# Blocks of 120 tokens laid end to end over the batches, weight chunks in one transfer, taps zeroed at batch starts

## The chip, the core and the metric

The kernel runs on one core of a Trainium2 chip. The metric is the device time of one launch in microseconds (us). Five engines work side by side, each through its own instructions in program order: PE (TensorE, matrix multiplies and transposes), DVE (VectorE), ACT (ScalarE), POOL (GpSimd) and SP (SyncE, which here only issues transfers). Transfers between DRAM and on-chip memory run on 16 DMA engines.

## The reference

Two steps follow each other. The first is a dynamic convolution: for each of 8 x 4160 tokens, eight heads of 24 channels each mix the last seven tokens (the taps) with softmaxed weights; before a batch's first token stand zeros. The second picks, in each batch, the 128 tokens of highest score, sends them through two expert matrices and adds the gated result.

```python
w = np.exp(weight_gen - max); w = w / (w.sum(-1) + 1e-9)          # (8, 4160, 8 heads, 7 taps)
x_pad = concat([zeros(B, 6, D), x], axis=1)                       # D = 192
out[b, s, h] = sum over k of w[b, s, h, k] * x_pad[b, s + k, h]   # 24 channels per head
scores = out @ w_gate
for b in range(8):
    top = argpartition(-scores[b], 128)[:128]
    ye = relu(out[b, top] @ w1) @ w2                              # 192 -> 1024 -> 192
    out[b, top] += sigmoid(scores[b, top])[:, None] * ye
```

## The kernel before

**Windows and blocks.** The output is cut into windows of `W` = 120 tokens. A window reads 128 rows of x: its 120 tokens and the six before them. Each batch has `NW` = 35 windows, the last with 80 tokens, so there are `TOT` = 280 windows, and `U` = 4 of them form one of `NU` = 70 blocks. A block of x is loaded by SP (`load_x`, L158) into one of `NST` = 5 staging tiles `xst`, cast to 16 bits by POOL (`cast_x`, L168) into one of `XR` = 24 tiles `x`, and there the six rows before a batch start are zeroed (L174).

**Weights.** The windows fall into three groups of two, three and three batches (70, 105 and 105 windows). In a group a window is a partition, and its tokens lie along the row, in five chunks of 24 tokens. `load_w` (L217) loads a chunk with two transfers for each batch, of 32 and of 3 partitions. For a chunk ACT computes the exponential (`sm_exp`, L235), DVE (first group) or POOL (`sm_den`, L249 or L252 to L256) the sum over taps, ACT its reciprocal (`sm_r`, L262 and L264), and DVE multiplies (`sm_norm`, L274). PE transposes the result (L293), and DVE or ACT copy it out as `wt` (L304, L306).

**The loop.** In iteration `s`, DVE builds the banded matrix of block `s + 2` (`band`, L728), PE multiplies block `s` (`conv`, L754), ACT copies block `s - 1` out of PSUM as `co` (L777), and SP stores it (`put`, L767). Beside that PE transposes x (`y_t`, L320) 1.49 blocks per iteration, so that all scores are known at iteration 46, long before block 69 is convolved; the transposed x is copied out (L329, L331) and multiplied by the gate (L343 to L349). After the scores come the search for the top 128 (DVE), and for each batch a gather, the experts and a scatter.

**The order.** It is written out by hand. `feed` issues loads of x and, once five are ahead, a cast; before the loop it is called until `XA` = 16 blocks are loaded and 11 cast. In the loop the loads are spread evenly up to iteration 43, and `cast_to` keeps the casts ahead of the transposes. `SM1`, `WT1`, `SM2` and `WT2` are the iterations of the softmax steps and weight transposes of the second and third groups. Each engine keeps this order: an instruction that waits holds everything behind it on its engine. Transfers from SP and ACT draw on eight completion semaphores in turn, so the queue also waits for the transfer that had the same semaphore before.

Of the kernel before, what the change touches and what calls it, by code (L numbers as in the profile page):

```python
# [33 lines left out]
XR = 24  # L34
# [8 lines left out]
def kernel(  # L43
# [17 lines left out]
    NW = -(-S // W)  # L61
    LAST = S - (NW - 1) * W
    TOT = B * NW
    NU = TOT // U
    assert NU * U == TOT
    GROUPS = ((0, 2), (2, 5), (5, 8))
    NWG = 3 * NW

# [31 lines left out]
def fast_path(  # L100
    ctx, tc, x_flat, wg_flat, moe_w_gate, moe_w1, moe_w2, out_flat, sc_d, cand_d, flag_i,
    B, S, F, CAP, N, SP, PPB, NW, LAST, TOT, NU, GROUPS, NWG, MUL,
# [29 lines left out]
    def row0(g):  # L132
        b, i = divmod(g, NW)
        return b * S + i * W - (K - 1)

    xst = {}

    def load_x(u):

        t = xsp.tile([P, U, D], FP32, tag="xst", name="xst")  # L140
        xst[u] = t
        g, end = u * U, (u + 1) * U
        while g < end:
            b = g // NW
            e = min(end, (b + 1) * NW)
            lo, hi = g, e
            if g == 0:
                nc.gpsimd.memset(t[0:K - 1, 0, :], 0.0)
                nc.sync.dma_start(out=t[K - 1:P, 0, :], in_=x_flat[0:P - (K - 1), :])
                lo += 1  # L150
            if e == TOT:
                hi -= 1
                j = hi - u * U
                r = min(P, N - row0(hi))
                nc.gpsimd.memset(t[:, j, :], 0.0)
                nc.sync.dma_start(out=t[0:r, j, :], in_=x_flat[row0(hi):row0(hi) + r, :])
            if hi > lo:
                nc.sync.dma_start(  # L158
                    out=t[:, lo - u * U:hi - u * U, :],
                    in_=ap_of(x_flat, x_flat.offset + row0(lo) * D,  # L160
                              [[D, P], [W * D, hi - lo], [1, D]]),
                )
            g = e

    def cast_x(u):
        t = xp.tile([P, U, D], FP16, tag="x", name=f"x{u}")
        xs[u] = t
        nc.gpsimd.tensor_copy(  # L168
            out=t.rearrange("p u d -> p (u d)"), in_=xst.pop(u).rearrange("p u d -> p (u d)")
        )  # L170
# [26 lines left out]
    def load_w(gi, ci, home=None):  # L197
        b0, b1 = GROUPS[gi]
# [4 lines left out]
        for b in range(b0, b1):  # L203
            p0 = (b - b0) * NW
            n = NW
            if b == B - 1 and t0 + nt > LAST:
                n = NW - 1
                lim = max(0, LAST - t0)
                nc.gpsimd.memset(t[96:(b1 - b0) * NW, 0:nt, :], 0.0)
                if lim > 0:  # L210
                    nc.sync.dma_start(
                        out=t[p0 + n:p0 + n + 1, 0:lim, :],
                        in_=wg_flat[None, b * S + n * W + t0:b * S + n * W + t0 + lim, :],
                    )
            cuts = [0, 32, n]
            for u, v in zip(cuts[:-1], cuts[1:]):
                nc.sync.dma_start(  # L217
                    out=t[p0 + u:p0 + v, 0:nt, :],
                    in_=ap_of(wg_flat, wg_flat.offset + (b * S + u * W + t0) * HK,
                              [[W * HK, v - u], [HK, nt], [1, HK]]),  # L220
                )
# [20 lines left out]

    def sm_den(gi, ci, eng):
# [4 lines left out]
        if eng == "v":  # L248
            nc.vector.tensor_reduce(out=d, in_=av[:, :, :, 0:K], axis=AX.X, op=ALU.add)  # L249
        else:  # L250
# [5 lines left out]
            nc.gpsimd.tensor_tensor(out=d, in0=s4[:, :, :, 0], in1=s4[:, :, :, 1], op=ALU.add)  # L256
        sm[(gi, ci)] = den
# [55 lines left out]
    y16 = ypl.tile([P, TOT, H], FP16, name="y16")  # L313
    ystate = {}

    def y_t(u):
        xf = xs[u].rearrange("p t d -> p (t d)")
        tp = ps_t.tile([P, M, P], FP16, tag="tps", name="xtps")
        for r in range(NT):
# [5 lines left out]
    def y_x(u, eng):  # L325
        tp = ystate.pop(u)
        xT = xtp.tile([P, NT, P], FP16, tag="xT", name="xT")
        if eng == "v":
            nc.vector.tensor_copy(out=xT[:, :, :], in_=tp[:, 0:NT, :])  # L329
        else:  # L330
            nc.scalar.copy(out=xT[:, :, :], in_=tp[:, 0:NT, :])  # L331
        ystate[u] = xT

    def y_d(u, cps, j):
# [4 lines left out]
        for r in range(NT):  # L339
# [12 lines left out]
    def y_e(us, cps):  # L352
        n = len(us) * U
# [10 lines left out]
    def score_t(gi):  # L364
        b0, b1 = GROUPS[gi]
        n = (b1 - b0) * NW
        w0 = b0 * NW
# [39 lines left out]
    def score_m(gi, j):  # L407
        b0, b1 = GROUPS[gi]
# [842 lines left out]
```

## Time and profile before

| | us |
|---|---|
| median of 3 runs | 295.83 (294.73 to 297.66) |
| the profiled execution | 295.27 |
| its span, first to last instruction | 293.5 |
| around the span | 1.8 |

The profile is of one execution. Busy times are those of single engines and overlap. A row's square bracket names the idle time of the engine just before the instruction and what ended it. The mean share of the 16 DMA engines counts the time that packets took, waiting on memory included, so it may pass 1.

### The profile page before, as it was taken

How to read it: one execution, taken by the hardware profiler on the slowest of the kernel's cores; microseconds unless marked ns; L12 is line 12 of the kernel's file. 1: busy time of each engine (PE TensorE's matmuls, PEld its weight loads, DVE VectorE, ACT ScalarE, POOL GpSimd, SP SyncE). 2: the span in 40 equal slices, each digit the busy share in tenths (PEclk: the TensorE clock that was granted, in tenths of full speed). 3: DMA queues.
4: the chain of work that ended last, by engine and by line, in shares of the span. 5: the costliest groups of instructions: out<-in, count | busy, mean ns of one | idle time of the engine just before them, and what ended most of it. 6: DMA issues, size and time to landing. Idle time of an engine off the chain costs nothing.

```text
span 293.5 us, 8921 instructions
## 1 busy us (share of the span) xinstructions
PE 171.8 (59%) x3627; PEld 159.0 (54%) x3627; DVE 226.2 (77%) x242; ACT 170.5 (58%) x331; POOL 155.7 (53%) x199
## 2 busy tenths in 40 slices
PE   0005731647499489464569869577581316679950
PEld 0005731647399489454569859577571214677740
DVE  3798953978979999955777989977989998797100
ACT  2874604869779638676589858665141851436720
POOL 5637339886624219846734533249561933864431
PEclk9999999975969855955557998855555555559965
DMA  3698899899899999997999998785934540747410
GB/s 103 162 273 239 205 272 249 227 337 325 246 308 337 278 256 290 253 256 207 317 322 344 334 310 252 211 270 151 170 87 104 162 135 10 191 129 212 132 40 21
DMA packets 78610, 64.04 MB, mean 218 GB/s; under 512 B 7261, under 2 KB 76718, under 8 KB 78564
## 3 DMA queue, kind: packets, MB, share of 16 engines
q1 hardware_dynamic: 76084, 61.05, 72.2%
q0 software_dynamic: 2032, 2.36, 3.8%
q8 instruction: 30, 0.49, 0.7%
q14 instruction: 16, 0.13, 0.2%
q10 hardware_dynamic: 448, 0.00, 0.1%
HBM read 37.70 MB, written 26.49 MB: 219 GB/s over the span
## 4 chain that ended last, share of the span: by engine, by line
DMA 29%; DVE 19%; PE 17%; POOL 13%; issue 12%; ACT 5%; SPq 1%; ACTq 1%; POOLq 0%; DVEq 0%
DMA xst<-in_x_dram 14%; DMA out_dram<-co 10%; PE sps L414 4%; POOL x L168 4%; PE cps L754 4%; DVE band__163 L728 4%; DVE sp L398 3%; DVE band__161 L728 3%; PE xtps L320 3%; DVE junk L555 3%; POOL s L252 2%; DVE band__162 L728 2%; ACT xT L331 2%; POOL out_dram L709 2%; PE wtps L293 2%
## 5 line engine op out<-in xcount | busy, mean ns | idle before, releaser
L168 POOL CAST x<-xst 128x768 f16<-128x768 f32 x70 | 62.6, 904 | 72.1 <-DMA xst<-in_x_dram 59.7
L777 ACT COPY co<-cps 128x768 f32<-128x768 f32 x70 | 56.1, 806 | 41.1 <-DMA out_dram<-co 17.2
L728 DVE TENSOR_TENSOR band__161<-wt,mask 128x3840 f16<-128x3840 f16 (+1 forms) x24 | 48.9, 2039 | 4.3 <-PE cps L754 4.2
L728 DVE TENSOR_TENSOR band__162<-wt,mask 128x3840 f16<-128x3840 f16 (+2 forms) x24 | 46.9, 1958 | 5.6 <-PE cps L754 5.6
L320 PE MATMUL xtps<-ident,x 128*128 128x128 f16 x420 | 43.7, 270 | 11.4 <-DVE xT L329 6.4
L728 DVE TENSOR_TENSOR band__163<-wt,mask 128x3840 f16<-128x3840 f16 (+2 forms) x24 | 46.4, 1935 | 2.1 <-PE cps L754 2.1
L331 ACT COPY xT<-xtps 128x768 f16<-128x768 f16 x56 | 44.7, 830 | 5.4 <-PE xtps L320 5.4
L320 PEld LDWEIGHTS <-x 128*128 128x128 f16 x420 | 33.9, 122 | 12.0 <-issue 6.6
L754 PE MATMUL cps<-x,band__162 128*128 128x24 f16 x736 | 23.5, 179 | 22.2 <-ACT y L354 16.8
L754 PEld LDWEIGHTS <-band__162 128*128 128x128 f16 x736 | 23.0, 103 | 23.7 <-issue 17.4
L754 PE MATMUL cps<-x,band__163 128*128 128x24 f16 x736 | 23.1, 179 | 15.3 <-ACT y L354 10.3
L754 PEld LDWEIGHTS <-band__163 128*128 128x128 f16 x736 | 22.8, 102 | 16.9 <-issue 15.2
L754 PEld LDWEIGHTS <-band__161 128*128 128x128 f16 x768 | 24.2, 104 | 14.0 <-DVE band__161 L728 9.9
L754 PE MATMUL cps<-x,band__161 128*128 128x24 f16 x768 | 24.4, 180 | 12.5 <-DVE band__161 L728 8.7
L274 DVE TENSOR_TENSOR amem<-amem,r 105x1536 f16<-105x1536 f16 (+1 forms) x15 | 18.2, 1210 | 15.1 <-ACT r L264 15.0
L293 PE MATMUL wtps<-ident,amem 105*128 105x105 f16 (+1 forms) x192 | 14.7, 247 | 23.8 <-DVE amem L274 17.6
L293 PEld LDWEIGHTS <-amem 105*128 105x128 f16 (+1 forms) x192 | 13.1, 125 | 25.0 <-DVE amem L274 18.5
L414 PE MATMUL sps<-sp,ident 105*105 105x240 f16 (+1 forms) x96 | 17.5, 352 | 8.0 <-DVE sp L398 5.7
L235 ACT ACTIVATE amem<-wraw 105x1344 f16<-105x1344 f32 (+1 forms) x13 | 17.1, 1315 | 8.5 <-DMA wraw<-in_weight_gen_dram 5.4
L414 PEld LDWEIGHTS <-ident 105*105 105x105 f16 (+1 forms) x96 | 14.7, 168 | 8.8 <-DVE sp L398 4.3
L398 DVE TENSOR_TENSOR sp<-amem,Y 105x1920 f16<-105x1920 f16 (+1 forms) x12 | 16.9, 1421 | 1.6 <-ACT Y L381 1.6
L252 POOL TENSOR_TENSOR s<-amem 105x768 f32<-105x768 f16 x10 | 14.7, 1466 | 4.7 <-ACT amem L235 4.6
(175 smaller groups left out, 375.7 us busy)
## 6 DMA issues: line engine op xcount, KB each, us to landing
xst<-in_x_dram SPq DMA_DIRECT2D x62, 384.0 KB
out_dram<-co SPq DMA_DIRECT2D x62, 360.0 KB
wraw<-in_weight_gen_dram SPq DMA_DIRECT2D x36, 168.0 KB
xst<-in_x_dram SPq DMA_DIRECT2D x6, 288.0 KB
out_dram<-co SPq DMA_DIRECT2D x4, 270.0 KB
xst<-in_x_dram SPq DMA_DIRECT2D x4, 192.0 KB
out_dram<-co SPq DMA_DIRECT2D x4, 180.0 KB
amem<-in_weight_gen_dram SPq DMA_DIRECT2D x4, 168.0 KB
```

The source lines that it names most:

```text
L168: nc.gpsimd.tensor_copy(out=t.rearrange("p u d -> p (u d)"), in_=xst.pop(u).rearrange("p u d -> p (u d)"))
L235: nc.scalar.activation(out=a_view(gi)[0:n, :, q0:q1, 0:K].rearrange("p c q k -> p q c k"), in_=wr[0:n, 0:nq * M, :].rearrange("p (q m) (h ...
L252: nc.gpsimd.tensor_tensor(out=s4, in0=av[:, :, :, 0:4], in1=av[:, :, :, 4:8], op=ALU.add)
L274: nc.vector.tensor_tensor(out=v, in0=v, in1=r2[0:n, 0:cq, :].rearrange("p (c q) b -> p c q b", q=nq)[:, :, :, None, :] .to_broadcast([n, M ...
L293: nc.tensor.transpose(out=tp[:, m, 0:n], in_=am[0:n, o:o + P], identity=ident16[0:n, 0:n])
L320: nc.tensor.transpose(out=tp[:, r, :], in_=xf[:, r * P:(r + 1) * P], identity=ident16[:, :])
L331: nc.scalar.copy(out=xT[:, :, :], in_=tp[:, 0:NT, :])
L398: nc.vector.tensor_tensor(out=sp[0:n], in0=ap_of(a0, am[0:n, o:o + 1].offset, [list(a0.ap[0]), [2 * H * Q * 8, 2], [Q * 8, H], [1, Q * 8]] ...
L414: nc.tensor.matmul(out=sps[0:n].rearrange("p m q k -> p m (q k)"), lhsT=ident16[0:n, 0:n], rhs=sp[0:n, :, h, :], start=(h == 0), stop=(h = ...
L728: eng.tensor_tensor(out=bt[:, o:o + n * H * BC].rearrange("p (c q m) -> p c q m", q=NQ, m=M), in0=wts[gi][:, l:l + n].rearrange("p w h m - ...
L754: nc.tensor.matmul(out=cps[:, w // 2, (w % 2) * D + h * G:(w % 2) * D + (h + 1) * G], lhsT=bt[:, o:o + P], rhs=xwin(si * U + w)[:, h * G:( ...
L777: nc.scalar.copy(out=co.rearrange("p (j w) d -> p j (w d)", w=2), in_=cts[si][:, :, 0:2 * D],)
```

## The change

Windows run through all 33,280 tokens without regard to batches. There are 278 of them (the last holds 40 tokens), and 70 blocks (the last holds two windows). The groups have 64, 112 and 102 windows. A weight chunk is loaded in one transfer of 64 or 112 partitions; in the third group it is one of 96 and one of 5 or 6, and for four of its chunks (before: two) POOL first zeroes the last rows. Since a window may now hold a batch start, the taps that reach over it are zeroed in the weights after the sum over taps: seven batch starts give six multiplies on DVE (`sm_start`) with masks that POOL builds at the start (`start_masks`). Zeroing x at batch starts goes. `XR` is 23, `XA` 12, and `SM1` and `WT1` are earlier. The gate's loads (`wcol`) are issued first, and x's first loads and the masks stand ahead of the other constants.

```diff
-XR = 24
+XR = 23
-    NW = -(-S // W)
-    LAST = S - (NW - 1) * W
-    TOT = B * NW
-    GROUPS = ((0, 2), (2, 5), (5, 8))
+    TOT = -(-N // W)
+    LAST = N - (TOT - 1) * W
+    NU = -(-TOT // U)
+    GB = (64, 176)
+    GROUPS = ((0, GB[0]), GB, (GB[1], TOT))
...
     def cast_x(u):
-        for j in range(U):
-            if (u * U + j) % NW == 0:
-
-                nc.gpsimd.memset(t[0:K - 1, j, :], 0.0)
...
     def load_w(gi, ci, home=None):
-        for b in range(b0, b1):
-            p0 = (b - b0) * NW
-            n = NW
...
-            cuts = [0, 32, n]
-            for u, v in zip(cuts[:-1], cuts[1:]):
+        n = w1 - w0
+        if w1 == TOT and t0 + nt > LAST:
+            lim = max(0, LAST - t0)
+            nc.gpsimd.memset(t[96:n, 0:nt, :], 0.0)
+            n -= 1
+            if lim > 0:
+                g = (w0 + n) * W + t0
+                nc.sync.dma_start(out=t[n:n + 1, 0:lim, :], in_=wg_flat[None, g:g + lim, :])
+
+        cuts = [0, n // 16 * 16] + ([n] if n % 16 else [])
+        for u, v in zip(cuts[:-1], cuts[1:]):
+            nc.sync.dma_start(
+                out=t[u:v, 0:nt, :],
+                in_=ap_of(wg_flat, wg_flat.offset + ((w0 + u) * W + t0) * HK,
+                          [[W * HK, v - u], [HK, nt], [1, HK]]),
+            )
...
+    def start_masks():
+
+        for (gi, q), ps in starts.items():
+            ts = []
+            for p in ps:
+                t = consts.tile([P, M, 8], FP16, name=f"bm{gi}_{q}_{p}")
+                nc.gpsimd.affine_select(
...
+                nc.gpsimd.affine_select(
...
+    def sm_start(gi, ci, eng):
+        n, q0, q1, nq, col, cq = dims(gi, ci)
+        for q in range(q0, q1):
+            if (gi, q) in bms:
+                v = a_view(gi)[0:n, :, q, :].rearrange("p (m h) k -> p m h k", h=H)
+                eng.tensor_tensor(
+                    out=v, in0=v,
+                    in1=bms[(gi, q)][0:n, :, None, :].to_broadcast([n, M, H, 8]), op=MUL,
+                )
...
             nc.vector.tensor_reduce(out=d, in_=av[:, :, :, 0:K], axis=AX.X, op=ALU.add)
+            sm_start(gi, ci, nc.vector)
...
     def sm_norm(gi, ci):
+        if gi and SE:
+            sm_start(gi, ci, nc.vector)
...
-    XA = 16
+    XA = 12
+    SE = 1
-    SM1 = (0, 1, 3, 5, 7)
-    WT1 = (11, 11, 11, 12, 12, 12, 13, 13)
+    SM1 = (0, 1, 3, 4, 6)
+    WT1 = (9, 9, 10, 10, 11, 11, 12, 12)
...
+    nc.scalar.dma_start(out=wcol[:, 0:1], in_=wgv[0:128, :])
...
     for ci in range(NWC):
         load_w(0, ci, None if ci < 3 else spare[:, ci - 3])
...
+    feed(NST - 1)
+    start_masks()
+    sel_consts()
+    ex_consts()
     gsel = consts.tile([P, 4, H], FP32, name="gsel")
```

**On ACT, at the very start** (`wcol` is the gate, `mask_s` a copy of the band's mask, `amem` the softmax memory), before:

```order
L80 ACT_TABLE_LOAD
L849 COPY mask_s<-mask 128x120
L852 DMA wcol<-in_moe_w_gate_dram 128x1
L853 DMA wcol<-in_moe_w_gate_dram 64x1
L854 DMA wcol<-in_moe_w_gate_dram 64x1
L855 DMA wcol<-in_moe_w_gate_dram 128x1
L235 ACTIVATE amem_128,emax<-wraw 70x3x64x7 x2
```

and with the change:

```order
L79 ACT_TABLE_LOAD
L854 DMA wcol<-in_moe_w_gate_dram 128x1
L855 DMA wcol<-in_moe_w_gate_dram 64x1
L856 DMA wcol<-in_moe_w_gate_dram 64x1
L857 DMA wcol<-in_moe_w_gate_dram 128x1
L889 COPY mask_s<-mask 128x120
L225 ACTIVATE amem_128,emax<-wraw 64x3x64x7 x2
```

The four issues moved from behind the copy of the mask, which waits for PE, to ahead of it.

**On POOL, the casts of x ahead of the second group's first sum over taps** (`s` and `den` are its steps). Before, the last seven of 13 casts stand here:

```order
L168 CAST x_339<-xst 128x768
L168 CAST x_343<-xst 128x768
L168 CAST x_347<-xst 128x768
L174 MEMSET x_347 6x192
L168 CAST x_352<-xst 128x768
L168 CAST x_356<-xst 128x768
L168 CAST x_360<-xst 128x768
L168 CAST x_447<-xst 128x768
L252 TENSOR_TENSOR s_506<-amem_129 105x768
L253 TENSOR_TENSOR s_506<-s_506 105x192x2
L256 TENSOR_TENSOR den<-s_506 105x192
```

and with the change the last three of nine:

```order
L164 CAST x_344<-xst 128x768
L164 CAST x_348<-xst 128x768
L164 CAST x_435<-xst 128x768
L283 TENSOR_TENSOR s_489<-amem_129 112x768
L284 TENSOR_TENSOR s_489<-s_489 112x192x2
L287 TENSOR_TENSOR den<-s_489 112x192
L164 CAST x_495<-xst 128x768
```

Four casts moved from ahead of the sum to behind it.

**On SP, around the third group's first two chunks** (`co` is a finished block, `xst` a load of x), before:

```order
L767 DMA out_dram<-co 120x4x192
L217 DMA wraw<-in_weight_gen_dram 32x1344
L217 DMA wraw<-in_weight_gen_dram 3x1344
L217 DMA wraw<-in_weight_gen_dram 32x1344
L217 DMA wraw<-in_weight_gen_dram 3x1344
L217 DMA wraw<-in_weight_gen_dram 32x1344
L217 DMA wraw<-in_weight_gen_dram 3x1344
L158 DMA xst<-in_x_dram 128x4x192 x2
```

and with the change:

```order
L804 DMA out_dram<-co 120x4x192
L207 DMA wraw<-in_weight_gen_dram 96x1344
L207 DMA wraw<-in_weight_gen_dram 6x1344
L154 DMA xst<-in_x_dram 128x4x192
L804 DMA out_dram<-co 120x4x192
L203 DMA wraw<-in_weight_gen_dram 1x896
L207 DMA wraw<-in_weight_gen_dram 96x1344
L207 DMA wraw<-in_weight_gen_dram 5x1344
L154 DMA xst<-in_x_dram 128x4x192
```

A chunk takes two or three places in the queue where it took six, and the transfers of the second chunk stand behind a zeroing on POOL.

## Rows read from the trace of the kernel before

**Rows 1.** The page: span, busy time by engine, and the DMA share in 40 slices.

```profile
span 293.5 us, 8921 instructions
PE 171.8 (59%) x3627; PEld 159.0 (54%) x3627; DVE 226.2 (77%) x242; ACT 170.5 (58%) x331; POOL 155.7 (53%) x199
DMA  3698899899899999997999998785934540747410
```

**Rows 2.** Stretches of the span: busy us of each engine, granted clock, DMA share, GB/s.

```profile
0.00:20.00 20.00, 0.28 (x1) 0.10 (x1) 13.07 (x18) 12.10 (x25) 9.70 (x36) 1.00 0.63 172
20.00:60.00 40.00, 19.30 (x402) 18.06 (x403) 30.74 (x24) 19.70 (x38) 27.00 (x30) 1.00 0.91 241
60.00:100.00 40.00, 29.64 (x718) 28.41 (x718) 34.27 (x23) 32.57 (x61) 20.78 (x26) 0.79 1.00 309
100.00:140.00 40.00, 25.75 (x530) 24.47 (x530) 32.65 (x26) 24.98 (x50) 22.71 (x26) 0.59 0.91 252
140.00:192.00 52.00, 38.64 (x901) 36.94 (x898) 43.94 (x33) 38.93 (x71) 22.21 (x27) 0.76 0.97 300
192.00:254.00 62.00, 32.08 (x679) 29.33 (x680) 55.35 (x103) 25.36 (x54) 36.62 (x30) 0.50 0.54 136
```

**Rows 3.** The waits: who waited for whom, us in total, times, longest.

```profile
POOL x L168 <- DMA xst<-in_x_dram: 59.7, 36, 5.2
ACT den L262 <- POOL den L256: 14.6, 6, 11.0
PE xtps L320 <- POOL x L168: 5.0, 2, 3.2
```

**Rows 4.** ACT in order of time: start, us, line, operation, idle time before.

```profile
4.72 0.26 ACT L849 COPY mask_s<-mask 128x120 f16<-128x120 f16 x1 [2.62 <-PE mask L848]
4.73 0.39 ACTq L852 DMA_DIRECT2D wcol<-in_moe_w_gate_dram  x1
6.36 0.92 ACTq L855 DMA_DIRECT2D wcol<-in_moe_w_gate_dram  x1
7.46 1.33 ACT L235 ACTIVATE amem<-wraw 70x1344 f16<-70x1344 f32 x1 [2.47 <-DMA wraw<-in_weight_gen_dram]
47.80 0.36 ACT L262 ACTIVATE den<-den 105x192 f32<-105x192 f32 x1 [10.96 <-POOL den L256]
```

**Rows 5.** POOL in order of time: the first, ninth, thirteenth and last cast, the first sum.

```profile
19.07 0.82 POOL L168 CAST x<-xst 128x768 f16<-128x768 f32 x1 [5.05 <-DMA xst<-in_x_dram]
35.70 0.83 POOL L168 CAST x<-xst 128x768 f16<-128x768 f32 x1 [2.37 <-DMA xst<-in_x_dram]
44.00 0.83 POOL L168 CAST x<-xst 128x768 f16<-128x768 f32 x1 [0.38 <-DMA xst<-in_x_dram]
44.80 1.47 POOL L252 TENSOR_TENSOR s<-amem 105x768 f32<-105x768 f16 x1
193.47 0.83 POOL L168 CAST x<-xst 128x768 f16<-128x768 f32 x1 [0.57 <-DMA xst<-in_x_dram]
```

**Rows 6.** The page on transfers: queue (packets, MB, share); issues, KB each.

```profile
q1 hardware_dynamic: 76084, 61.05, 72.2%
xst<-in_x_dram SPq DMA_DIRECT2D x62, 384.0 KB
wraw<-in_weight_gen_dram SPq DMA_DIRECT2D x36, 168.0 KB
wraw<-in_weight_gen_dram SPq DMA_DIRECT2D x34, 15.8 KB
```

**Rows 7.** Groups of instructions by line and form: busy us, mean ns of one, idle before.

```profile
L274 DVE TENSOR_TENSOR amem<-amem,r 105x1536 f16<-105x1536 f16 x10 | 12.9, 1290 | 15.0 <-ACT r L264 15.0
L209 POOL MEMSET wraw<- 9x1344 f32 x2 | 2.4, 1212 | 6.1 <-DMA out_dram<-co 6.0 <-POOL x L168 0.2
L840 POOL TENSOR_SCALAR_AFFINE_SELECT band__161<-ones 128x128 f16<-128x128 f16 x1 | 0.3, 292 | 0.1
```

**Rows 8.** The chain that ended last, around the last loads of x.

```profile
185.67 6.29 DMA xst<-in_x_dram
192.07 0.84 POOL x L168
198.62 1.82 PE ytps L370 x8
```

More of the change, by code (lines that the diff above doesn't have):

```diff
@@ L141, in load_x @@
         xst[u] = t
[L142 to L163, printed above, removed]
+        lo, hi = u * U, u * U + nwin(u)
+        if lo == 0:
+            nc.gpsimd.memset(t[0:K - 1, 0, :], 0.0)
+            nc.sync.dma_start(out=t[K - 1:P, 0, :], in_=x_flat[0:P - (K - 1), :])
+            lo += 1
+        if hi == TOT:
+            hi -= 1
+            j = hi - u * U
+            r = min(P, N - row0(hi))
+            nc.gpsimd.memset(t[:, j, :], 0.0)
+            nc.sync.dma_start(out=t[0:r, j, :], in_=x_flat[row0(hi):row0(hi) + r, :])
+        nc.sync.dma_start(
+            out=t[:, lo - u * U:hi - u * U, :],
+            in_=ap_of(x_flat, x_flat.offset + row0(lo) * D,
+                      [[D, P], [W * D, hi - lo], [1, D]]),
+        )
     def cast_x(u):
@@ L318, in y_t @@
         tp = ps_t.tile([P, M, P], FP16, tag="tps", name="xtps")
-        for r in range(NT):
+        for r in range(ntr(u)):
             nc.tensor.transpose(
@@ L328, in y_x @@
         if eng == "v":
-            nc.vector.tensor_copy(out=xT[:, :, :], in_=tp[:, 0:NT, :])
+            nc.vector.tensor_copy(out=xT[:, 0:ntr(u), :], in_=tp[:, 0:ntr(u), :])
         else:
-            nc.scalar.copy(out=xT[:, :, :], in_=tp[:, 0:NT, :])
+            nc.scalar.copy(out=xT[:, 0:ntr(u), :], in_=tp[:, 0:ntr(u), :])
         ystate[u] = xT
@@ L338, in y_d @@
         yps = cps[:, 0, o:o + U * H].rearrange("p (w h) -> p w h", h=H)
-        for r in range(NT):
+        for r in range(ntr(u)):
             q, w = divmod(r, 3)
@@ L352, in y_e @@
     def y_e(us, cps):
-        n = len(us) * U
+        n = sum(nwin(u) for u in us)
         nc.scalar.copy(
@@ L724, in band_part @@
         while g < end:
-            gi = next(i for i, (b0, b1) in enumerate(GROUPS) if g < b1 * NW)
-            n = min(end, GROUPS[gi][1] * NW) - g
-            l, o = g - GROUPS[gi][0] * NW, (g - si * U) * H * BC
+            gi = next(i for i, (b0, b1) in enumerate(GROUPS) if g < b1)
+            n = min(end, GROUPS[gi][1]) - g
+            l, o = g - GROUPS[gi][0], (g - si * U) * H * BC
             eng.tensor_tensor(
@@ L739, in band @@
     def band(si):
-        g, end = si * U, (si + 1) * U
+        g, end = si * U, si * U + nwin(si)
         if si in PBS:
@@ L750, in conv @@
         cps = ps_c.tile([P, 2, 512], FP32, tag="cps", name="cps")
-        for w in range(U):
+        for w in range(nwin(si)):
             for h in range(H):
@@ L849, in fast_path, with feed @@
     nc.scalar.copy(out=mask_s[:, :], in_=mask[:, :])
-    wcol = consts.tile([P, 3], FP32, name="wcol")
-    wgv = moe_w_gate.rearrange("(d o) -> d o", o=1)
-    nc.scalar.dma_start(out=wcol[:, 0:1], in_=wgv[0:128, :])
-    nc.scalar.dma_start(out=wcol[0:64, 1:2], in_=wgv[128:192, :])
-    nc.scalar.dma_start(out=wcol[64:128, 1:2], in_=wgv[0:64, :])
-    nc.scalar.dma_start(out=wcol[:, 2:3], in_=wgv[64:192, :])
+    loaded, casted = [0], [0]
+    def feed(n):
+        for _ in range(n):
+            if loaded[0] < NU:
+                load_x(loaded[0])
+                loaded[0] += 1
+                if loaded[0] - casted[0] >= NST:
+                    cast_x(casted[0])
+                    casted[0] += 1
+    feed(NST - 1)
+    start_masks()
+    sel_consts()
+    ex_consts()
     gsel = consts.tile([P, 4, H], FP32, name="gsel")
@@ L868, in fast_path @@
         )
-    loaded, casted = [0], [0]
-    def feed(n):
-        for _ in range(n):
-            if loaded[0] < NU:
-                load_x(loaded[0])
-                loaded[0] += 1
-                if loaded[0] - casted[0] >= NST:
-                    cast_x(casted[0])
-                    casted[0] += 1
-    feed(NST - 1)
-    sel_consts()
-    ex_consts()
     sm_exp(0, 0)
@@ L1014, in fast_path @@
     s = s + EG
-    blast = [((b + 1) * NW - 1) // U for b in range(B)]
+    blast = [((b + 1) * S - 1) // W // U for b in range(B)]
     ya = {}
```

140 lines of the change are left out of this document (76 added, 64 removed).

## The prediction

> **What bounds the kernel now.** I read the page first: no engine is busy all the time, DVE most with 77%, while the DMA share stands at eight or nine tenths from the second slice to the 28th and then falls [rows 1]. So there are two regimes, and the stretches show them [rows 2]. Up to 192 us the core moves 172 x 20 + 241 x 40 + 309 x 40 + 252 x 40 + 300 x 52, or 51.1 MB: nearly all of x, all weights, and the stores so far. Here the DMA share is 0.91 to 1.00, except in the first 20 us (0.63). From 192 us on the share is 0.54 and DVE is busy 55.35 of 62 us. The hinge is the last load of x: in the chain it is issued at 185.67 us, lands 6.29 us later, is cast, and the last scores leave PE at 198.62 us [rows 8]. The last cast begins at 193.47 us [rows 5], and what follows, 293.5 - 193.5, is 100 us of search, experts and remaining blocks in an order that the change leaves iteration for iteration. **So the question is by how much the last cast comes earlier.**
>
> Two things hold it back. One is a hole in the opening: ACT stands idle 10.96 us, from 36.84 to 47.80 us, before the first reciprocal of the second group [rows 4], waiting for POOL's sum, and the total of such waits is 14.6 us [rows 3]. POOL is late because in its order 13 casts stand ahead of that sum and each waits for its load: POOL waited 59.7 us for loads of x [rows 3]. Behind the reciprocal on ACT stand the copies of finished blocks, so PE and the stores wait too. The other is rate: the two stretches with weight chunks run at 241 and 252 GB/s, the two without at 309 and 300 [rows 2].
>
> **The change part by part.**
>
> *The start, -2.0 us.* ACT copies the mask at 4.72 us, then issues four loads of the gate up to 6.36 + 0.92 = 7.28 us, and the first exponential follows at 7.46 us [rows 4]. With the issues ahead of the copy, in the 2.62 us in which ACT waited for PE, the exponential can begin at 4.98 us if the first chunk is there. That is up to -2.5; I take -2.4, and 0 is the other end, if the chunk is later. One mask multiply (priced below) falls into this part on DVE: +0.4. POOL's 14 selects and one multiply for the masks cost at most 15 x 0.292 = 4.4 us, by a row of twice their size [rows 7]; POOL idled 5.05 us before the first cast [rows 5], which covers them. If x lands 5 us earlier than before, that cover is gone and the first casts wait for the masks, which then eat part of that lead.
>
> *The hole, -8.2 us.* Only nine casts stand ahead of the first sum now. The ninth cast began at 35.70 us, the sum began after the thirteenth at 44.80 us [rows 5]; a cast takes 0.83 us, so the sum could have begun at 36.6 us, 8.2 us earlier. This leaves 10.96 - 8.2 = 2.8 us of ACT's wait. What is late next is the last of the group's five sums, which stands behind 17 casts (before: 21) one iteration earlier.
>
> *The four blocks that are no longer loaded ahead, +5.1 us.* They must go through later, beside stores. 4 x 384 KB [rows 6] is 1.57 MB, and from 60 to 100 us the DMA engines have a share of 1.00 at 309 GB/s [rows 2], so nothing is free there: 1.57 MB / 309 GB/s = 5.1 us. The other end is 0, if holes in the queue take them up.
>
> *Weight chunks in one transfer, -3.5 us.* Each batch's 35 windows went as 168.0 KB and 15.8 KB [rows 6], so a chunk of the third group took six places in a queue that has eight completions in turn, three of them with almost no data. Now it takes two or three. If the third group's stretch (100 to 140 us, 252 GB/s, 10.1 MB) rises halfway to the 300 GB/s of the stretch without chunks [rows 2], it takes 10.1 / 276 = 36.5 us: -3.5. The ends are 0 and, at 309 GB/s, -7.3. The second group's stretch is the one with the hole; I count nothing twice. The Trainium skill ("DMA: Bandwidth & Descriptors", section "Why a DMA increments its semaphore by 16 and not by 1") says that a transfer runs on the largest number of engines up to 16 that divides its partitions, and from the lowest up, so 3 partitions burden three engines. No view here shows the engine of a packet. By that rule, with 72.2% x 16 x 293.5 us / 76,084 packets = 45 ns for a mean packet of 802 bytes [rows 1, 6], or 0.30 us for 5,376, the lowest three engines would shed (15 - 5) x 0.30 = 3.0 us in the third group, and the sum would be half a microsecond smaller.
>
> *Mask multiplies, +1.1 us.* Six on DVE, 512 elements each. The nearest row has 1,536 elements in 1.29 us [rows 7]; a third is 0.43, the whole row the upper end. One is counted above. The other five are 2.2 us, and DVE is busy 30.74 and 32.65 of 40 us where they fall [rows 2], so I put half on the path. The ends are 0 and 5 x 1.29 = 6.5.
>
> *One buffer of x fewer, +0.8 us.* The last cast must wait for block 46 instead of 45 to be convolved; its 0.83 us [rows 5] then stands between that and the last transposes. Earlier casts have slack of an iteration or more.
>
> *At nothing.* Four zeroings instead of two cost POOL 2 x 1.212 us more [rows 7] and eight small ones go; POOL waits for loads most of that time. The last block has half a band, but after 254 us the end hangs on gathers and scatters.
>
> Sum: -2.0 - 8.2 + 5.1 - 3.5 + 1.1 + 0.8 = -6.7. Against the profiled execution's 295.27 us that is 288.6; the median of the runs is 0.6 us above it. I say **288.5 us**.
>
> **The rivals.**
>
> *It is given back (293.8 us).* If the 51.1 MB set the time of the last cast and rates don't change, the opening's gain turns into a longer queue. Then only the empty first 20 us help: a share of 0.80 instead of 0.63 gives 3.4 us, less 1.9 for multiplies and buffer, -1.5. For it speaks the share of 1.00 from 60 to 100 us; against it that the hole keeps stores out of the mix just where the rate is low.
>
> *All of it stays (279.6 us).* The four blocks fit into holes and the third group's stretch reaches 309 GB/s: -2.0 - 8.2 - 7.3 + 1.9 = -15.6. For it: shares of 0.91 on both stretches with chunks. Against it: DVE, busy 34.27 of 40 us at 60 to 100 us, leaves little room there.
>
> *x comes too late (302 us, slower).* Loads of x are issued closer to their use: at iteration 20 the casts are three blocks ahead of the transposes instead of five, and each of four chunks of the third group makes SP wait for a zeroing on POOL, which stands behind casts. PE already waited for casts twice, 5.0 us in all, 3.2 at the longest [rows 3]. Without the -3.5 the sum is -3.2; it passes +3 with two such waits of 3.2 us, and three of them give 295.27 - 3.2 + 9.6 = 301.7. Against it: such waits come only at the end of the loads so far. In a sentence beside it, the Trainium skill's advice (same page, "Rules for kernel authors") is to issue a transfer early and wait late, which the change goes against; the trace agrees only in part, since the early loads made the hole.
>
> **How the numbers follow.** I give the forecast 0.53, given back 0.20, all stays 0.14, x too late 0.13. A measurement of this kernel can't tell less than about 1% from no change, so same is 292.9 to 298.8 us. Faster: forecast and all stays, with a little of given back, 0.69. Same: most of given back and the edge of x too late, 0.19. Slower: 0.12. The range 279 to 298 us takes in the forecast with its ends, given back, and most of all stays; what lies outside is x too late and some outcomes below, together below 0.2.
>
> **What would show it.** First exponential near 5 us; ACT's wait for POOL's first sum below 4 us; first copy of a finished block near 29 us instead of 31; GB/s above 265 in the third group's stretch; last cast near 187 us; from there to the end 100 us as before. If the hole closes but the last cast stays near 192 us, given back is right; if PE's waits for casts pass 10 us, x comes too late. The forecast is wrong if the part behind the last cast changes by more than 2 us.

## The result, and the profile after

| | before | after |
|---|---|---|
| median of 4 runs | 295.94 us (294.73 to 297.66) | 279.76 us (275.8 to 282.34) |
| profiled execution | 295.27 | 279.23 |
| its span | 293.5 | 277.5 |

The ratio is 0.937, with an interval of 0.925 to 0.950: 16 us faster, more than double the forecast of 6.7 us. Slow runs, over 1.5% above the fastest of their kernel (here 280.29 and 282.34 us), are left out of the ratios and of the times in the experiments; the other two runs after have a median of 277.5 us.

The page after, with the lines that answer to [rows 1], and the chain's shares by engine:

```profile
span 277.5 us, 8755 instructions
PE 168.9 (61%) x3605; PEld 154.0 (55%) x3605; DVE 231.1 (83%) x246; ACT 170.0 (61%) x331; POOL 163.4 (59%) x208
DMA  6999999999899999898999978967563430747410
DVE 33%; PE 17%; issue 16%; DMA 14%; POOL 11%; ACT 5%; SPq 1%; POOLq 1%; DVEq 0%; ACTq 0%
```

The DMA engines stand at seven to nine tenths from the second slice to the 26th, where before it was from the third to the 27th, in longer slices. In the chain before, DMA had 29% and DVE 19%; now DVE has 33% and DMA 14%. The stretches after, columns as in [rows 2]:

```profile
0.00:20.00 20.00, 0.28 (x1) 0.10 (x1) 15.56 (x20) 12.96 (x27) 16.86 (x53) 1.00 0.93 225
20.00:60.00 40.00, 23.74 (x546) 21.98 (x546) 39.06 (x28) 29.38 (x57) 31.23 (x32) 0.78 1.04 292
60.00:100.00 40.00, 30.18 (x652) 27.86 (x652) 39.08 (x29) 26.02 (x46) 16.65 (x17) 0.71 0.99 296
100.00:140.00 40.00, 28.87 (x635) 26.90 (x634) 35.08 (x25) 32.90 (x67) 32.12 (x34) 0.63 0.98 300
140.00:180.00 40.00, 31.33 (x770) 30.23 (x770) 35.46 (x27) 28.22 (x49) 14.60 (x19) 0.80 0.96 301
```

All stretches from 20 to 180 us now move 292 to 301 GB/s; 241 and 252 were the low ones before. Only the first 20 us stay below, at 225 instead of 172. DVE is busy 39 of 40 us in two stretches.

The same stretch does not hold the same work before and after. SP issues the third group's chunks from 94.6 us on before, and from 80.6 us on now, the last of the five at 105 us. So the rate along these loads is read over 36 us from their first issue, before:

```profile
94.00:130.00 36.00, 25.94 (x563) 24.57 (x560) 32.41 (x25) 23.34 (x47) 20.11 (x24) 0.68 0.97 271
```

and after:

```profile
80.00:116.00 36.00, 28.77 (x617) 25.64 (x615) 32.28 (x26) 24.61 (x47) 23.00 (x24) 0.65 1.04 307
```

The waits after, that answer to [rows 3]:

```profile
POOL x L164 <- DMA xst<-in_x_dram: 36.0, 27, 4.3
ACT den L295 <- POOL den L287: 6.6, 7, 2.3
PE xtps L358 <- POOL x L164: 9.8, 7, 2.8
```

ACT's longest wait for POOL's sum fell from 11.0 to 2.3 us, and PE's waits for casts rose from 5.0 to 9.8 us. ACT after, in order of time, against [rows 4]:

```profile
4.73 0.26 ACT L889 COPY mask_s<-mask 128x120 f16<-128x120 f16 x1 [2.63 <-PE mask L888]
5.17 1.33 ACT L225 ACTIVATE amem<-wraw 64x1344 f16<-64x1344 f32 x1 [0.18 <-DMA wraw<-in_weight_gen_dram]
29.25 0.80 ACT L814 COPY co<-cps 128x768 f32<-128x768 f32 x1 [2.60 <-PE cps L792]
34.58 0.36 ACT L295 ACTIVATE den<-den 112x192 f32<-112x192 f32 x1 [1.12 <-POOL den L287]
```

and POOL after, against [rows 5]: the ninth cast, the first sum behind it, and the last cast.

```profile
30.78 0.83 POOL L164 CAST x<-xst 128x768 f16<-128x768 f32 x1 [3.08 <-DMA xst<-in_x_dram]
31.57 1.47 POOL L283 TENSOR_TENSOR s<-amem 112x768 f32<-112x768 f16 x1
179.83 0.51 POOL L164 CAST x<-xst 128x384 f16<-128x384 f32 x1 [1.85 <-PE cps L792]
```

The first exponential comes 2.3 us earlier, the first reciprocal of the second group at 34.58 instead of 47.80, the last cast at 179.83 instead of 193.47 us. The transfers of the second and third groups' chunks, from the same page, against [rows 6]:

```profile
wraw<-in_weight_gen_dram SPq DMA_DIRECT2D x5, 588.0 KB, 10.3
wraw<-in_weight_gen_dram SPq DMA_DIRECT2D x5, 504.0 KB, 8.6
```

Where the time went shows in the starts (us) of the copies that end a block, one row of the trace each (L777 before, L814 after, shifted by a few lines in the experiments):

| block | before | after | XA 16 | cut | cut, XA 16 | tiny loads |
|---|---|---|---|---|---|---|
| 0 | 31.27 | 29.25 | 29.24 | 31.39 | 30.98 | 31.62 |
| 3 | 54.31 | 42.21 | 48.87 | 44.32 | 55.88 | 46.19 |
| 8 | 69.96 | 56.95 | 64.25 | 64.83 | 71.39 | 67.29 |
| 20 | 109.64 | 99.31 | 106.50 | 103.42 | 113.56 | 108.90 |
| 33 | 157.20 | 142.25 | 149.59 | 150.67 | 157.13 | 163.84 |
| 46 | 194.97 | 180.05 | 186.68 | 188.04 | 195.79 | 202.65 |

Before against after, 2.0 us are gained up to block 0, 10.1 more up to block 3, 0.9 up to block 8; 2.7 are given back by block 20; 4.6 are gained up to block 33; nothing up to 46. From the last cast to the end it is 97.7 us, where it was 100.0.

### The profile page after: what moved, and what is told of

It is laid out like the page before. It is cut to its first block, busy times and chain, and to the rows that moved or that the text cites. A ratio compares the mean times of both kernels' runs of the same rounds, so it can differ in the third digit from the quotient of the medians.

```text
span 277.5 us, 8755 instructions
## 1 busy us (share of the span) xinstructions
PE 168.9 (61%) x3605; PEld 154.0 (55%) x3605; DVE 231.1 (83%) x246; ACT 170.0 (61%) x331; POOL 163.4 (59%) x208
## 4 chain that ended last, share of the span: by engine, by line
DVE 33%; PE 17%; issue 16%; DMA 14%; POOL 11%; ACT 5%; SPq 1%; POOLq 1%; DVEq 0%; ACTq 0%
DVE amem L309 5%; DMA wraw<-in_weight_gen_dram 5%; DVE band__162 L766 5%; PE cps L792 5%; DVE band__163 L766 4%; DMA xst<-in_x_dram 4%; DVE sp L435 4%; PE sps L451 3%; DVE band__161 L766 3%; DMA out_dram<-co 3%; DVE junk L593 3%; PE wtps L328 3%; PE xtps L358 2%; POOL s L283 2%; POOL out_dram L747 2%
## 5 line engine op out<-in xcount | busy, mean ns | idle before, releaser
L814 ACT COPY co<-cps 128x768 f32<-128x768 f32 x70 | 55.6, 799 | 31.1 <-PE cps L792 10.9
L766 DVE TENSOR_TENSOR band__161<-wt,mask 128x3840 f16<-128x3840 f16 (+2 forms) x24 | 47.9, 1996 | 2.4 <-PE cps L792 2.3
L766 DVE TENSOR_TENSOR band__162<-wt,mask 128x3840 f16<-128x3840 f16 (+1 forms) x23 | 46.8, 2035 | 1.7 <-PE cps L792 1.6
L766 DVE TENSOR_TENSOR band__163<-wt,mask 128x3840 f16<-128x3840 f16 (+1 forms) x23 | 46.3, 2012 | 0.1
L369 ACT COPY xT<-xtps 128x768 f16<-128x768 f16 (+1 forms) x56 | 44.2, 821 | 2.3 <-PE xtps L358 2.3
L328 PE MATMUL wtps<-ident,amem 64*128 64x64 f16 (+2 forms) x192 | 13.8, 238 | 28.2 <-DVE amem L309 23.4
L451 PE MATMUL sps<-sp,ident 64*64 64x240 f16 (+2 forms) x96 | 17.9, 356 | 10.3 <-DVE sp L435 6.1
L309 DVE TENSOR_TENSOR amem<-amem,r 64x1536 f16<-64x1536 f16 (+2 forms) x15 | 22.6, 1506 | 0.5 <-ACT r L297 0.2
L225 ACT ACTIVATE amem<-wraw 112x1344 f16<-112x1344 f32 (+2 forms) x13 | 17.2, 1321 | 8.5 <-DVE sp L435 6.0
L451 PEld LDWEIGHTS <-ident 64*64 64x64 f16 (+2 forms) x96 | 14.6, 165 | 11.9 <-issue 6.8
L341 ACT COPY wt<-wtps 128x816 f16<-128x816 f16 (+2 forms) x17 | 13.9, 826 | 10.2 <-PE wtps L328 10.2
L435 DVE TENSOR_TENSOR sp<-amem,Y 64x1920 f16<-64x1920 f16 (+2 forms) x12 | 17.5, 1470 | 1.6 <-ACT Y L418 1.6
```

The costliest lines, as they stand in the source:

```text
L225: nc.scalar.activation(out=a_view(gi)[0:n, :, q0:q1, 0:K].rearrange("p c q k -> p q c k"), in_=wr[0:n, 0:nq * M, :].rearrange("p (q m) (h ...
L309: nc.vector.tensor_tensor(out=v, in0=v, in1=r2[0:n, 0:cq, :].rearrange("p (c q) b -> p c q b", q=nq)[:, :, :, None, :] .to_broadcast([n, M ...
L328: nc.tensor.transpose(out=tp[:, m, 0:n], in_=am[0:n, o:o + P], identity=ident16[0:n, 0:n])
L341: nc.scalar.copy(out=dst, in_=src)
L369: nc.scalar.copy(out=xT[:, 0:ntr(u), :], in_=tp[:, 0:ntr(u), :])
L435: nc.vector.tensor_tensor(out=sp[0:n], in0=ap_of(a0, am[0:n, o:o + 1].offset, [list(a0.ap[0]), [2 * H * Q * 8, 2], [Q * 8, H], [1, Q * 8]] ...
```

## The experiments

Two parts of the change are tried first, as the ones that may carry so much: the x blocks no longer loaded ahead (`XA`), and the weight chunk in one transfer. Of the second there are two theories: the pieces cost because each takes a turn in the queue, whatever its size; or because pieces of 3 partitions load the DMA engines unevenly. The rivals outside are the gate's earlier loads and DVE. Each kernel is the changed one with one edit, unless said; the kernel before took 295.2 to 295.6 us on the same chips.

**The control (c0_after).** The changed kernel again.

> The changed kernel again, beside the three below on one chip: 276 to 282 us, 0.93 to 0.95 of the kernel before.

Measured 278.30 us, ratio 0.942 (0.937 to 0.947). Its first stretch with weights, which the others are held against, with the columns of [rows 2]:

```profile
20.00:60.00 40.00, 24.75 (x546) 22.94 (x546) 39.05 (x28) 29.47 (x59) 31.40 (x32) 0.70 1.07 300
```

**Four blocks loaded ahead again (e3_xa16).**

```diff
-    XA = 12
+    XA = 16
```

> The changed kernel with 16 blocks of x loaded ahead again (13 casts ahead of the second group's first sum). Theory B: the hole on ACT is back at 6 to 9 us and the time is 285 to 288 us. Theory A: with whole chunks the casts come sooner, the hole is under 4 us and the time rises by at most 3 us, since the blocks loaded ahead needn't be loaded later.

285.96 us, ratio 0.971 (0.964 to 0.978), 7.7 above the control. Its same stretch:

```profile
20.00:60.00 40.00, 20.66 (x446) 18.95 (x447) 31.43 (x25) 22.59 (x44) 28.24 (x29) 0.70 0.98 272
```

and its first reciprocal of the second group on ACT:

```profile
42.10 0.36 ACT L295 ACTIVATE den<-den 112x192 f32<-112x192 f32 x1 [8.67 <-POOL den L287]
```

The hole is back, 8.67 us of it, and with it the stretch falls to 272 GB/s. Block 3 comes 7.1 us later than in the control (41.73), block 8 7.8 (56.48), block 20 7.5 (99.03), block 33 7.7 (141.87). So what the hole costs is not recovered: loading four blocks more ahead spares nothing later.

**The kernel before with fewer blocks ahead (b1_xa12).** In the kernel before, 12 for `XA` = 16.

> The kernel before with 12 blocks of x loaded ahead instead of 16, all else as before. If the order alone carries its 7.7 us (what 16 blocks cost the changed kernel), this is 287 to 290 us. If fewer blocks ahead help only beside whole chunks, it is 293 us or more.

292.91 us, ratio 0.991 (0.987 to 0.996): 2.7 us below the kernel before on its chip. The same step is worth a third of what it is worth in the changed kernel.

**The old cuts (e1_split3).** Chunks in pieces like the old ones, at the same places in the order.

```diff
-        cuts = [0, n // 16 * 16] + ([n] if n % 16 else [])
+        sizes = {64: (32, 3, 26, 3), 112: (32, 3, 32, 3, 32, 3, 7),
+                 102: (32, 3, 32, 3, 28, 4), 101: (32, 3, 32, 3, 28, 3)}[n]
+        cuts = [0]
+        for z in sizes:
+            cuts.append(cuts[-1] + z)
```

> The changed kernel with each weight chunk cut again into four to seven transfers of mostly 32 and 3 partitions. Theory A (a chunk in one transfer is what raised the rate in the second and third groups' stretches from 241 and 252 to 292 and 300 GB/s): those rates fall below 270 again and the time is 286 to 292 us. Theory B (four blocks of x fewer ahead of the first sum did it, the transfers little): within 2 us of the changed kernel.

288.19 us, ratio 0.980 (0.973 to 0.988), 9.9 above the control. The stretch:

```profile
20.00:60.00 40.00, 19.60 (x446) 18.47 (x447) 34.62 (x26) 23.64 (x46) 26.92 (x27) 0.75 0.85 236
```

Here the rate falls to 236 GB/s at a share of 0.85, though ACT waits only 2.3 us in all for POOL's sums there: the queue itself is not kept full. What SP waited for before its loads of x (L154) up to 60 us, us in total, times, longest, in this kernel:

```profile
SPq L154 <- DMA xst<-in_x_dram: 10.5, 5, 3.5
SPq L154 <- POOL x L164: 1.9, 2, 1.5
```

and in the changed kernel:

```profile
SPq L154 <- POOL x L164: 14.2, 14, 3.3
SPq L154 <- DMA xst<-in_x_dram: 1.9, 2, 1.2
```

With whole chunks a load waits for a staging tile that POOL must empty; with pieces it waits for earlier transfers to land, which fits completions that are taken in turn. Against the control, block 0 is 1.9 us late, block 8 8.4, block 20 4.4, block 33 8.8: time is lost while the second group's pieces go, half of it is regained, and it is lost again around the third group's. The stretch from 100 to 140 us does not fall below 270 GB/s, as was expected: it moves 293. But along the third group's loads the rate is lower than in the control, over 36 us from the first issue, in this kernel:

```profile
87.00:123.00 36.00, 27.85 (x583) 24.88 (x580) 32.13 (x25) 24.08 (x49) 23.82 (x24) 0.64 0.99 273
```

and in the control:

```profile
80.00:116.00 36.00, 28.55 (x614) 25.62 (x613) 32.28 (x26) 24.69 (x47) 22.07 (x23) 0.65 1.05 303
```

**Both undone (e11_split3_xa16).** The two edits above together.

> The changed kernel with both undone: chunks cut into 32 and 3, and 16 blocks of x loaded ahead. With this the four combinations are there. If the two parts are all of the gain, it is 293 to 297 us, as the kernel before. If they simply add up (10.4 and 7.7 us over 278.3), 296 us; if the new layout itself (aligned groups, fewer pieces at batch ends, the start) has a share, it is below 293 us.

293.71 us, ratio 0.992 (0.987 to 0.996). Its stretch:

```profile
20.00:60.00 40.00, 16.59 (x346) 15.32 (x347) 25.95 (x22) 17.67 (x33) 24.89 (x24) 1.00 0.84 224
```

| us | `XA` 16 | `XA` 12 | gain |
|---|---|---|---|
| chunks cut | 293.7 | 288.2 | 5.5 |
| chunks whole | 286.0 | 278.3 | 7.7 |
| gain | 7.7 | 9.9 | |

The two parts make 15.4 us together, and each is worth 2.2 us more beside the other. All else in the change (blocks over batch edges, groups, multiplies, buffer, gate, earlier `SM1` and `WT1`) is left with the 0.8% between this kernel and the kernel before. With 12 blocks ahead the rest may be worth a little more: e1_split3 stands at 0.980 and b1_xa12 at 0.991, with intervals that just overlap. The earlier `SM1` and `WT1` were not tried alone.

**Even pieces (e2_split16).** Every piece has 16 partitions, with as many or more pieces.

```diff
-        cuts = [0, n // 16 * 16] + ([n] if n % 16 else [])
+        cuts = list(range(0, n // 16 * 16 + 1, 16)) + ([n] if n % 16 else [])
```

> The changed kernel with each chunk cut into transfers of 16 partitions, four to seven of them. If the small uneven transfers burden some DMA engines (the engines' share is what counts), this is as fast as the changed kernel within 2 us. If it is the number of places in a queue with eight completions, it is as slow as the cut into 32 and 3, 286 us or more.

292.93 us, ratio 0.993 (0.990 to 0.997); the stretch at 20 to 60 us moves 227 GB/s. Without the pieces of 3 partitions the kernel is slower than with them. By the rule of the Trainium skill cited in the prediction ("DMA: Bandwidth & Descriptors", section "Why a DMA increments its semaphore by 16 and not by 1") even pieces would have shed the burden on the lowest engines; in this kernel shedding it gained nothing that outweighs five more transfers.

**Two pieces (e6_split2), four pieces (e8_split4).** In multiples of 16, and of 32 partitions.

```diff
-        cuts = [0, n // 16 * 16] + ([n] if n % 16 else [])
+        cuts = [0, (n // 16 + 1) // 2 * 16, n // 16 * 16] + ([n] if n % 16 else [])   # e6
+        cuts = list(range(0, n // 16 * 16, 32)) + [n // 16 * 16] + ([n] if n % 16 else [])   # e8
```

> The changed kernel with each chunk in two transfers of multiples of 16 partitions. If each further place in the queue costs alike (seven places cost 14.6 us), two cost about 2.4 us: 280 to 282 us. If only many places hurt, because they fill most of the eight completions, it is within 1 us of the changed kernel.

> The changed kernel with chunks of 112 in four transfers (three of 32, one of 16), of 64 in two, of 102 in four. Two places cost nothing, seven cost 14.6 us. If the cost sets in once most of eight completions hold weights, four places cost under 3 us: 278 to 281 us. If it grows evenly from the third place on, 284 us.

278.31 us (0.943, 0.935 to 0.950) and 279.87 us (0.949, 0.942 to 0.956). Both intervals overlap the control's: up to four pieces cost at most little.

**Turns without data (e5_tiny).** Whole chunks, and behind each three (first group) or six loads of 16 x 4 bytes into a tile that nothing reads.

```diff
+        for _ in range(6 if gi else 3):
+            j = ntiny[0]
+            ntiny[0] += 1
+            nc.sync.dma_start(
+                out=tiny[:, j:j + 1],
+                in_=ap_of(wg_flat, wg_flat.offset + w0 * W * HK, [[W * HK, 16], [1, 1]]),
+            )
```

> The changed kernel with whole chunks, and behind each chunk three (first group) or six loads of 16 x 4 bytes into a scratch tile that nobody reads: the same data, but as many places in the queue as seven pieces of 16. If places alone cost (the wait for one of eight completions and SP's time to issue), it is 288 to 293 us. If it is the cutting of the data itself, it is within 2 us of the changed kernel.

302.94 us, ratio 1.027 (1.021 to 1.033), 24.6 above the control, slower than the kernel before and well above the 288 to 293 us expected. SP's issues from the start (start, us):

```profile
0.83 0.58 SPq L209 DMA_DIRECT2D wraw<-in_weight_gen_dram  x1
1.47 1.75 SPq L217 DMA_DIRECT2D tiny<-in_weight_gen_dram  x3
5.04 0.48 SPq L209 DMA_DIRECT2D wraw<-in_weight_gen_dram  x1
```

the line's time to land, us:

```profile
DMA to landing us min/median/max: 2.6/4.3/6.4
```

and the stretch:

```profile
20.00:60.00 40.00, 19.33 (x426) 17.78 (x427) 33.97 (x27) 21.26 (x42) 27.37 (x27) 0.73 0.81 225
```

Such a load of 64 bytes takes some 0.5 us of SP's time here and lands 4.3 us after its issue in the median. The weights move in the same pieces as in the control, and the rate is 225 instead of 300 GB/s. So transfers with almost no data are enough to cost much. Their number is not all of the price: e2_split16 has 70 transfers more than the control and loses 14.6 us, these 75 lose 24.6, and why is open. SP's waits before its loads of x (L154) up to 60 us, in this kernel:

```profile
SPq L154 <- DMA xst<-in_x_dram: 6.2, 5, 1.9
SPq L154 <- DMA wraw<-in_weight_gen_dram: 3.1, 3, 1.4
```

These are 9.3 us for earlier transfers to land, where the control has 2.6. So waits for a turn are a part of the price; how much SP's issues are was not told apart.

**One group's chunks cut (e14_split_g1, e12_split_g2, e13_split_g3).** As e1_split3, in the first, second or third group alone; here what the edit of the first adds to that of e1_split3.

```diff
+        if gi != 0:
+            cuts = [0, n // 16 * 16] + ([n] if n % 16 else [])
```

> The changed kernel with only the first group's five chunks cut into 32, 3, 26 and 3. If the start's 2.0 us rest on whole chunks, the first finished block comes near 31.4 us instead of 29.4 and the time is 279.5 to 281 us; if a late start is made up behind it, as when the gate's loads were issued late, 278 to 279 us.

> The changed kernel with only the second group's five chunks cut into 32 and 3. If the prediction's failed step is that it gave these nothing, the stretch from 20 to 60 us falls from 300 to below 260 GB/s and the time is 282 to 285 us. If the second group's cuts cost nothing, as the prediction had it, 278 to 279.5 us.

> The changed kernel with only the third group's five chunks cut into 32 and 3. The prediction's 3.5 us for them gives 281 to 282.5 us. If the cost of the cuts lies in the opening alone, 278 to 279.5 us.

280.12 us (0.951, 0.944 to 0.958), 279.75 us (0.951, 0.941 to 0.961) and 279.70 us (0.948, 0.941 to 0.955): 1.8, 1.5 and 1.4 above the control, each with an interval that overlaps the control's, and 4.7 in sum where all three cost 9.9. The first group's time lies where it was expected, with block 0 at 30.53 and not 31.4 us; the second and third group's cuts alone stay below the 282 and 281 us that were expected if they are costly. The second group's rate does fall below 260 GB/s, but the time that its cuts lose is partly regained, as its two stretches show:

```profile
20.00:60.00 40.00, 22.22 (x484) 20.59 (x484) 33.46 (x26) 24.73 (x47) 26.66 (x27) 1.00 0.88 244
60.00:100.00 40.00, 31.18 (x678) 28.75 (x679) 39.27 (x29) 28.88 (x52) 18.31 (x22) 0.80 1.05 326
```

244 GB/s while the pieces go, then 326, above what any stretch of the changed kernel moves. The third group's cuts alone have, along their loads:

```profile
78.00:114.00 36.00, 28.19 (x581) 24.93 (x581) 32.29 (x26) 24.31 (x47) 21.59 (x22) 0.67 0.96 274
```

That is as low as before the change (271), against 303 in the control, and still the time is only 1.4 us longer. By the number of transfers and tiny loads that carry or follow the weights, the cuts fall roughly in one order:

| kernel | weight transfers | us above the control |
|---|---|---|
| control | 21 | 0 |
| e6_split2 | 36 | 0.0 |
| e14_split_g1 | 36 | 1.8 |
| e13_split_g3 | 41 | 1.4 |
| e8_split4 | 51 | 1.6 |
| e12_split_g2 | 51 | 1.5 |
| e1_split3 | 86 | 9.9 |
| e2_split16 | 91 | 14.6 |
| e5_tiny | 21 + 75 | 24.6 |

The price is small up to 51 and then grows faster than the number.

**The gate's loads behind the mask's copy again (e4_wcol_late).** The four issues stand behind the copy on ACT, as before the change.

```diff
-    nc.scalar.dma_start(out=wcol[:, 0:1], in_=wgv[0:128, :])
...
     # behind the copy of the mask
+    nc.scalar.dma_start(out=wcol[:, 0:1], in_=wgv[0:128, :])
...
```

> The changed kernel with the gate's four loads issued behind the mask copy again, as before. The prediction gave the start 2.0 us for that move: 280 to 281 us, first exponential near 7.4 us. The cut into 32 and 3 speaks against it: there the gate came early and the first finished block came as late as before (31.4 us), since the second exponential waited for its chunk; by that the move is worth under 1 us, 278 to 279.5 us.

278.31 us (0.939, 0.929 to 0.949), not to be told from the control. The first finished block comes at 30.77 instead of 29.48 us, block 20 at 99.49 against 99.03.

**DVE relieved (e7_pad_act, e10_dve_less).** e7 zeroes the eighth taps of the second softmax memory on ACT; e10 also gives ACT the copies of the transposed x and of the second group's weights.

```diff
-    XV = 5
+    XV = 70                                   # e10 alone
...
+        if i:
+            nc.scalar.copy(out=a_view(i)[:, :, :, K], in_=src)
+        else:
+            nc.vector.tensor_copy(out=a_view(i)[:, :, :, K], in_=src)
...
-    wt_moves(1, WT1, "ssvssvsv")
+    wt_moves(1, WT1, "ssssssss")              # e10 alone
```

> The changed kernel with the zeroing of the second softmax memory's eighth taps (2.30 us on DVE at 20.4 us, ahead of the first copies of weights) done on ACT, which idles 2.04 us there. If DVE's chain sets the opening, the first finished block comes 1.5 to 2.3 us earlier and the time is 275.5 to 277 us. If the DMA queue sets the pace after it, the gain is given back: 278 us.

> The changed kernel with the eighth taps zeroed on ACT (276.6 us as such), and 13 of 14 copies of transposed x and three copies of weights moved from DVE to ACT. DVE was busy 78 of 80 us from 20 to 100 us; this takes about 6 us off it there and puts 8 on ACT. If DVE sets the pace there, 271 to 274 us; if the DMA queue does (share 0.99 to 1.04), 275.5 to 277.5 us.

276.56 us (0.937, 0.930 to 0.945) and 277.03 us (0.935, 0.929 to 0.942); both intervals overlap the control's. The first finished block, expected 1.5 to 2.3 us earlier in e7 if DVE's chain sets the opening, came 1.0 us later there (30.49). The two middle stretches of e10:

```profile
20.00:60.00 40.00, 25.03 (x546) 23.35 (x546) 35.17 (x27) 32.50 (x59) 28.96 (x32) 0.81 1.03 281
60.00:100.00 40.00, 33.42 (x702) 30.03 (x703) 33.51 (x23) 33.14 (x57) 20.73 (x21) 0.76 1.04 310
```

DVE has 33.51 us of 40 at 60 to 100 us, where the changed kernel had 39.08, and the kernel gains nothing that can be told apart, at a DMA share of 1.03 and 1.04. So DVE's work alone does not set the pace there. What does was not shown: the DMA share is as high, but e3_xa16 has 0.98 at 272 GB/s, so a share near one is no ceiling of the rate. No version beat the changed kernel by more than the intervals.

## Why the prediction came out too small

**What bounds it, and the hinge: right in the main.** 13.6 of the 16.0 us of the profiled executions are the earlier last cast. The part behind it, "100 us as before", shrank by 2.3 us, just beyond the 2 us that were named as a sign of being wrong. The copy of the last block begins 21.2 us before the end before and 20.2 after, so 1.0 us of it lies behind that copy, with a last block of two windows; the rest lies ahead of it, and neither was tried alone. Two readings were loose, and nothing rests on them: the DMA share of [rows 1] is 6 tenths in the second slice, 7 in the 19th and 26th and 5 in the 28th, and 198.62 us is where the last transposes of [rows 8] begin.

**The start, -2.0: right in size, its cause shared.** The first exponential came at 5.17 us (near 5 said), block 0 at 29.25 (near 29 said). But the earlier loads of the gate are not all of it: with them late again block 0 comes 1.3 us later, with the first group's chunks cut 1.0 us later (30.53), and neither can be told from the control in the end. In e1_split3 the first exponential is as early, and the second waits for its chunk:

```profile
4.90 1.33 ACT L229 ACTIVATE amem<-wraw 64x1344 f16<-64x1344 f32 x1
8.78 1.33 ACT L229 ACTIVATE amem<-wraw 64x1344 f16<-64x1344 f32 x1 [2.46 <-DMA wraw<-in_weight_gen_dram]
```

**The hole, -8.2: right.** Nine casts stand ahead of the sum, the first wait is 1.12 us and the longest of the line 2.3. In e3_xa16, which puts the casts back, the wait is 8.67 us and the first reciprocal of the second group comes 8.0 us after the control's (42.10 against 34.11). Against the kernel before it came 13.2 us earlier, more than the casts alone give.

**"The four blocks that are no longer loaded ahead, +5.1 us": this step failed.** It took the bytes that leave the opening as a debt due from 60 to 100 us, where "nothing is free". The runs show no debt: against e3_xa16 the lead of the control is 7.1 us at block 3 and 7.7 at block 33. An estimate from the two rates says where the bytes went: at 300 instead of 272 GB/s, the 40 us with the hole carry 1.1 MB more, against the 1.57 MB that left the opening. The net of the two steps is -7.7 us beside whole chunks and -5.5 beside cut ones, not -8.2 + 5.1 = -3.1. The other end that was kept for this term, 0 "if holes in the queue take them up", was the right one.

**"Weight chunks in one transfer, -3.5 us": the mechanism was right, the term mis-sized.** It named the cause, transfers with almost no data in a queue of eight turns. Along the third group's loads the rate rose from 271 to 307 GB/s, where a rise from 252 to 276 was taken. (The stretch from 100 to 140 us, at 300 GB/s, does not show it: most of these loads now lie ahead of it.) But it gave the second group nothing: "the one with the hole; I count nothing twice". The low rate there had two causes, and each is seen alone: the hole without cuts gives 272 GB/s (e3_xa16), the cuts without the hole 236 (e1_split3), both 224 (e11_split3_xa16). The whole of the term is -9.9 us beside 12 blocks ahead and -7.7 beside 16. Cuts in one group alone cost 1.4 to 1.8, so it can't be divided between the groups; they cost most where they are many. Why the price climbs so steeply beyond 51 transfers stays open, and so does how much of it is SP's time for issues and how much the wait for a turn. Together the two parts give -15.4 us, where the sum had -8.2 + 5.1 - 3.5 = -6.6.

**Multiplies, +1.1, and buffer, +0.8: not tried alone.** With the layout and the earlier `SM1` and `WT1` they lie within the 0.8% that is left when both other parts are undone. The multiply was priced right for the median (0.43 us), not for each:

```profile
L267 DVE TENSOR_TENSOR amem<-amem,bm x6: 418/426/1953, 14.5 to 126.0; 112x512 f16<-112x512 f16 x3, 102x512 f16<-102x512 f16 x2, 64x512 f16<-64x512 f16 x1
```

**The rivals.** "All of it stays" (279.6 us) is what happened in time, but the agreement is in part luck: it had -7.3 us for the third group and nothing for the second, where the third group's cuts alone cost 1.4 us and all cuts together 9.9. What spoke against it, DVE's little room, did not matter: relieving it gave nothing that can be told apart (e10_dve_less). "Given back" is ruled out by the lead that e3_xa16 never makes good. "x comes too late" has a trace of truth, PE's waits for casts of 9.8 us, just below the 10 named, but they are short (2.8 at most) and the last cast came earlier all the same.

## What to carry to other kernels

When a stretch is slow for two reasons, price each by itself and let both count: taking them as one gain ("I count nothing twice") hid much of this one. Bytes that a change moves out of the opening are a debt only if no hole closes with it, so ask first what the queue could carry in the time that the change frees. Read a rate along the loads that it is meant to price, not in a fixed stretch: after a change that stretch may hold other work. And count transfers, not bytes alone: where completions are taken in turn, a load of 64 bytes takes its place as a large one does, and 75 of them cost this kernel some 25 us.

## What was not expected of the hardware

One normalising multiply of DVE took 0.96 us with no instruction on POOL beside it, and another of the same form 4.25 us (4.25 in the control too). DVE in order of time, in the changed kernel:

```profile
40.96 0.96 DVE L309 TENSOR_TENSOR amem<-amem,r 112x1536 f16<-112x1536 f16 x1
55.64 4.25 DVE L309 TENSOR_TENSOR amem<-amem,r 112x1536 f16<-112x1536 f16 x1
```

and POOL beside the second:

```profile
55.41 0.59 POOL L287 TENSOR_TENSOR den<-s 112x192 f32<-112x192 f32 x1
55.95 3.13 POOL L164 CAST x<-xst 128x768 f16<-128x768 f32 x4
```

The four casts lie within the multiply's time. The Trainium skill ("SBUF — State Buffer", section "SBUF: two separate sides") says that DVE and GpSimd share a pair of ports under an exclusive lock that lasts a whole instruction. The rows agree with that in so far as the long multiply begins beside POOL's sum and ends only after the casts; they do not show who held the ports, and no run here moved the casts away. So DVE's 39 of 40 busy us may hold time in which it only waited, and a busy share near one is not by itself a bound.

The same strided zeroing took ACT twice what it takes DVE. In e7_pad_act on ACT, and in the changed kernel on DVE (ns min, median, max):

```profile
L868 ACT COPY amem<-zero x1: 4464/4464/4464, 19.1 to 19.1; 128x960 f16<-128x960 f16 x1
```

```profile
L866 DVE COPY amem<-zero x2: 2286/2294/2301, 1.1 to 20.4; 128x960 f16<-128x960 f16 x2
```
